# Five small moves in the order of an attention and feed-forward kernel: warming products, first loads, squares, output stores, one cast

## The chip, the cores and the metric

The kernel runs on one core of a Trainium2 chip. The metric is the device time of one execution in microseconds (us). A core has five engines that run side by side, each through its own list of instructions in order: TensorE (PE: matrix products, with its weight loads shown as PEld), VectorE (DVE), ScalarE (ACT), GpSimd (POOL) and SyncE (SP), which here issues nearly all DMA transfers. An instruction that has to wait holds up everything that stands behind it on its engine.

## The reference

```python
def reference(A_x, A_wqkv, A_wo, B_x, B_w1, B_w3, B_w2):
    xn = layernorm(A_x)                                   # 2048 tokens, D = 512
    q, k, v = split(xn @ A_wqkv)                          # 32 heads of 16
    p = softmax(where(0 <= i - j < 256, q @ k.T / 4, -1e9))
    s = (p @ v) @ A_wo
    h = silu(xn @ B_w1) * (xn @ B_w3)                     # F = 1792
    g = silu(h @ B_w2)
    return A_x + s * g                                    # float32 in and out
```

## The kernel before, in words

Every float32 operand of a large product is scaled by a power of two and written as the sum of two float16 parts (hi and lo), and three products (hi·hi, lo·hi, hi·lo) stand for one. The power of two for a block of weights comes out of the weights themselves: their squares are summed (`squares`, on ACT at L249 or on DVE at L251), the sums are cast to bfloat16 (`cast`, L261, on DVE), a small product with ones spreads them over the partitions (`powers`, L280 or L285, on PE), and a chain of small DVE instructions (L291 or L294 to L304) makes the scale. Then the weights are scaled and cut: on ACT and DVE (`split`, L333, L334) or on ACT and POOL (`split_pool`, L342, L343, L345).

The 2048 tokens go in four stretches of 512 (t = 0 to 3), the heads in four groups of eight (g). At the start the first stretch of x is normalised, turned on PE (L493) and cut into XH (ACT, L496) and XL (DVE, L501). `project` (L597) makes the queries (k = 0) and keys (k = 1) of a group, cuts them (L614 on ACT, L618 on DVE) and stores them to DRAM; `fetch` (L641) loads them back in the layout of the attention, keys into `KA` and queries into `qa`. `value` (L567, L570) makes the values. Attention runs by units (t, g, p), where p takes half of a group's heads: `pass1` (L665 on PE, L679 on DVE) finds each row's maximum, `pass2` (L746 scores, L756 exponentials on ACT, L774 the product with the values) does the rest.

The feed-forward part is the filling between these batches: `gate_up` (L1036) for the 14 blocks of 128 columns of w1 and w3, `down` (L1261) for w2, and a form with fewer products for the last two stretches (L1179). In the first stretch the blocks are also loaded (L868, L913), measured two at a time (`measure`; `measure_down` for w2, L923) and cut. `total` (L1313) makes the final product with wo and the stores of the output (L1324).

PSUM is used as two banks `m` for dense products (`bank()` takes them in turn), two double banks `s` (`scores_bank()`) and one `po`. A product into a bank waits until the reader of the bank's previous content is done.

What sets the order: PE's instructions stand in the order in which the code is written. `later(n, f)` puts a piece of work n steps ahead, a step being a batch of attention or a piece of dense work. `beside_scores(n, f)` attaches a scale's small products to a pass1 row, n steps ahead. DVE, ACT, POOL and SP get their order from a scheduler that goes by priorities and its own estimate of when inputs are there, so an edit in one place can move instructions in another. The places of the change:

- `keep_busy(4)` at L1561 runs four products of ones into a bank `m` while the cuts of x are being made; `k00` and `q00` at L1564 are the first two projections, `k00` into an `s` bank.
- `later(1, lambda: fetch(0, 0))` at L1573 loads the first keys and queries in four transfers of 192 KB, each with four heads.
- `qk[3][0]()` at L1589 loads the query and key weights of group 3 in two transfers (L395); `later(6, qk[3][1])` takes their squares.
- At L1369 `measure(6, 1)`, the squares of blocks 6 and 7, is put 5 steps later.
- At L267 the cast of squares taken one per `apart` steps comes at `apart * (len(parts) + 1) + 1`. That is 6 steps for the blocks (four parts, apart 1) and 11 for wo (four parts, apart 2).
- At L1329 the output store comes 4 steps after its product, for all but the last stretch.

Of the kernel before, what the change touches and what calls it, by code (L numbers as in the profile page):

```python
# [83 lines left out]
def tile_block(ctx: ExitStack, tc: tile.TileContext, x, wqkv, wo, w1, w3, w2, out):  # L84
# [59 lines left out]
    def later(n, f):  # L144
        made_so_far[0] += 1
        queue.append((now[0] + n, made_so_far[0], f))
# [16 lines left out]
    def bank(shape, dtype=F32):  # L163

        open_bank[0] = b = 1 - open_bank[0]
        return psm.tile(shape, dtype, name=f"m{b}", tag=f"m{b}", bufs=1)

    def scores_bank():

        return pss.tile([P, 2, 512], F32, name="s")  # L170
# [11 lines left out]
    def beside_scores(n, f):  # L182

        later(n, lambda: besides.insert(0, f))
# [55 lines left out]
    def squares(parts, on_act=0, apart=0):  # L240


        ssq = small.tile([P, len(parts)], F32, name="ssq")

        def one(i, raw):

            sq = ppool.tile([P, D], BF16, name="sqa" if i < on_act else "junk", bufs=1)
            if i < on_act:
                nc.scalar.activation(sq, raw, AF.Square, accum_out=ssq[:, i:i + 1])  # L249
            else:  # L250
                nc.vector.tensor_tensor_reduce(out=sq, in0=raw, in1=raw, scale=1.0, scalar=0.0,  # L251
                                               op0=ALU.mult, op1=ALU.add, accum_out=ssq[:, i:i + 1])
        for i, raw in enumerate(parts):
            if apart:
                later(apart * (i + 1), lambda i=i, raw=raw: one(i, raw))
            else:
                one(i, raw)
        sb = small.tile([P, len(parts)], BF16, name="sb")

        def cast():  # L260
            lasts["cast"] = nc.vector.tensor_copy(sb, ssq)  # L261
        def behind_bank():

            with tc.issue_after(lasts["emptied"].ins) if "emptied" in lasts else nullcontext():
                cast()
        if apart:
            later(apart * (len(parts) + 1) + 1, behind_bank)  # L267
        else:
            cast()
        return sb  # L270
# [310 lines left out]
    def project(t, g, k, terms=(range(3),), scores_bank=False):  # L581


        cell = {}

        parts = ([[(c, i) for c in (2 * half, 2 * half + 1) for i in range(3)] for half in range(2)] if len(terms) == 1
                 else [[(c, i) for i in group for c in range(NC)] for group in terms])

        def part(n):
            assert turned[t] == 4  # L590
            w = WQ[t, g, k]
            xh, xl = X[t]
            if n == 0:
                cell["pp"] = pss.tile([P, 2, TW], F32, name="s")[:, 0, :] if scores_bank else bank([P, TW])
            for c, i in parts[n]:
                a, b = ((0, xh), (1, xh), (0, xl))[i]
                nc.tensor.matmul(cell["pp"], w[:, (a * NC + c) * P:(a * NC + c + 1) * P], b[:, c, :], start=(c, i) == parts[0][0],  # L597
                                 stop=(c, i) == parts[-1][-1])
            if n < len(parts) - 1:
                return  # L600
            if t == 0:
                def store():
                    with behind_load():
                        nc.sync.dma_start(dWQ[g, k], w)
                    give(w, after=8)
                later(45, store)
            else:
                give(w)
            pp = cell["pp"]
            both = take(F16)  # L610
            B = both.rearrange("p (a t) -> p a t", a=2)
            s = QS / (XS * WS)
            with urgent():
                nc.scalar.activation(B[:, 0, :], pp, AF.Copy, scale=s)  # L614

            def rest():
                with urgent():
                    lasts["emptied"] = nc.vector.scalar_tensor_tensor(B[:, 1, :], pp, s, B[:, 0, :], op0=ALU.mult, op1=ALU.subtract)  # L618
                d = (dQ, dK)[k][g][:, :, t * TW:(t + 1) * TW]
                if k == 0:  # L620
                    nc.sync.dma_start(d[:, 0:2, :], B[:, 0:1, :].to_broadcast([P, 2, TW]))
                    nc.sync.dma_start(d[:, 2, :], B[:, 1, :])
                else:
                    nc.sync.dma_start(d[:, 0:2, :], B)
                    nc.sync.dma_start(d[:, 2, :], B[:, 0, :])
                give(both, after=4)
            later(1, rest)
        return opening([(len(l), lambda n=n: part(n)) for n, l in enumerate(parts)])
# [2 lines left out]
        WQ[t, g, k] = w = take(F16)  # L631
        nc.sync.dma_start(w, dWQ[g, k])

    def fetch(t, g):
        QA[t, g] = qa = qpool.tile([P, 4, TW], F16, name="qa")
        ka = keys(t, g)
        c0 = 0 if t else 2 * P
        for dst, d in ((ka[:, :, c0:], dK[g][:, :, t * TW - 2 * P + c0:(t + 1) * TW]),
                       (qa, dQ[g][:, :, t * TW:(t + 1) * TW])):
            for r in range(2):  # L640
                lasts["load"] = nc.sync.dma_start(dst[64 * r:64 * r + KR],  # L641
                                  d[64 * r:64 * r + 64].rearrange("(a d) i t -> (d i) a t", d=DH))

# [224 lines left out]

    measured = set()

    def measure(f, apart=0):

        raws = [RAW.pop(f + i) for i in range(2)]
        sb = squares([raws[0][0], raws[1][0], raws[0][1], raws[1][1]], on_act=4 if f > 2 else 2, apart=apart)

        def scale(s=None):
            pp = small.tile([P, 2, 2], F32, name="pp")
            pi = small.tile([P, 2, 2], F32, name="pi")  # L880
            return then(s, powers(sb, 4, pp.rearrange("p a b -> p (a b)"), pi.rearrange("p a b -> p (a b)"), s),
                        lambda: rest(pp, pi))

        def rest(pp, pi):
            ff = slice(f, f + 2)
            nc.vector.tensor_scalar(sg_scale[:, ff], pp[:, 0, :], 0.5 / (WS * XS), None, op0=ALU.mult)
            nc.vector.tensor_mul(p13[:, ff], pp[:, 0, :], pp[:, 1, :])
            measured.update((f, f + 1))

            def cut(i, k):  # L890
                if k == 0:
                    WF[0, f + i] = [[None, None], WF.pop((0, f + i), [None, None])[1]]
                WF[0, f + i][0][k] = a = take(F16)
                split_pool(a[:, 0:D], a[:, D:], raws[i][k], pi[:, k, i:i + 1])
                give(raws[i][k], after=5)
            for i in range(2):
                for k in range(2):
                    later(((1, 2, 4, 6) if f < 8 else (1, 5, 9, 13))[2 * i + k], lambda i=i, k=k: cut(i, k))
        if started:
            beside_scores(8, scale)  # L900
        else:
            later(10 if apart else 6, scale)

# [389 lines left out]
    def total(t, b):  # L1293
# [4 lines left out]
        def part(half):  # L1298
# [16 lines left out]
            if half:  # L1315
                with urgent():
                    lasts["emptied"] = nc.vector.scalar_tensor_tensor(y, ps, sc["y"], y, op0=ALU.mult, op1=ALU.mult)
                if t == NT - 1:
                    nc.vector.tensor_add(y, y, XR[t, b])
                else:  # L1320
                    halves(nc.gpsimd.tensor_add, y, y, XR[t, b])

                def store():
                    nc.sync.dma_start(out[r, :], y)  # L1324
                    give(y, XR[t, b], after=30)
                if t == NT - 1:
                    store()
                else:
                    later(4, store)  # L1329
                if b == 3:  # L1330
                    give(*(OT[t, g] for g in range(NG)))
        return opening([(6, lambda h=h: part(h)) for h in range(2)])
# [22 lines left out]
    def feed_forward():  # L1355
# [4 lines left out]
        for t in range(NT):  # L1360
            for f in range(FB):
                if t == 0:
# [3 lines left out]
                    elif f + LEAD == FB - 1:  # L1366
                        pieces += [(0, lambda f=f: load(0, f)) for f in range(FB - 2, FB)]
                    if f % 2 and f + 3 < FB:
                        pieces.append((0, lambda f=f + 3: later(5, lambda: measure(f, 1)) if f == 6 else measure(f, 1)))  # L1369
                    pieces += [(0, lambda f=f: load_down(0, f)) for f in range(f + 2 if f else 0, min(f + 3, FB))]  # L1370
                    for m in range(f + 1 if f else 0, min(f + 2, FB)):
                        k = next(k for k, (_, f1) in enumerate(GROUPS) if m < f1)
# [158 lines left out]
        nc.gpsimd.memset(KA[2][:, a, :].bitcast(F32), TWO_ONES)  # L1531


    def keep_busy(n):
        ps = bank([P, 4, P])
        for _ in range(n):
            nc.tensor.matmul(ps, onesb, onesb.unsqueeze(1).to_broadcast([P, 4, P]), start=True, stop=True)

# [19 lines left out]
        flush()  # L1558
    with tc.issue_after(lasts["hi"].ins), tc.issue_after(lasts["x"].ins):
        qk[1][1]()  # L1560
    keep_busy(4)  # L1561


    k00, q00 = (project(0, 0, k, ((0,), (1,), (2,)), k) for k in (1, 0))  # L1564
    run([k00[0], q00[0], k00[1]])
    qk[1][2]()
    with tc.issue_after(lasts["scale"].ins):
# [2 lines left out]
    qk[1][3]()  # L1570
    with tc.issue_after(lasts["hi"].ins):
        run([k00[2], q00[2]])
    later(1, lambda: fetch(0, 0))  # L1573
    k01 = project(0, 1, 1, ((0, 2), (1,)))
    run(k01[:1])
    wv[2]()
# [4 lines left out]
    sc["o"] = scaled(SQ["wv"][3], OS / WS, "so")  # L1581
    with tc.issue_after(lasts["hi"].ins):
        measure(0)
    run(project(0, 1, 0, scores_bank=True))
    later(1, lambda: fetch(0, 1))
    run(value(0, True))
    qk[2][1]()
# [89 lines left out]
```

## Time and profile before

| | |
|---|---|
| Time, median of 3 runs | 811.51 us (811.10 to 811.94) |
| The profiled execution, its own time | 811.24 us |
| Its span, first to last instruction | 809.4 us |
| PE busy | 793.7 us (98%) |
| DVE busy | 631.2 us (78%) |
| ACT busy | 392.1 us (48%) |
| POOL busy | 377.1 us (47%) |
| DMA queue of SP, share of 16 engines | 54.6% |
| Granted TensorE clock, mean | 1.00 |

The span lies 1.8 us below the execution's own time, which has the start and the end around it. Lines of a timeline below give start in us, duration in us, engine, line, operation, output and inputs, shapes and, in brackets, the engine's idle time just before with what ended it.

### The profile page before, as it was taken

Reading aid. Unit: us, or ns where it says so; the run is one execution under the profiler, and the core shown is the slowest. Engines: PE = TensorE matmul, PEld = TensorE weight load, DVE = VectorE, ACT = ScalarE, POOL = GpSimd, SP = SyncE. Lnnn points to the kernel's source line nnn. Section 1 sums busy time; section 2 is a strip of 40 time slices with the busy share of each in tenths; the row PEclk is TensorE's granted clock in tenths of the full one; section 3 lists DMA queues with packets and bytes.
Section 4 is the critical chain, followed back from the end, with each engine's and each line's share of the span. In section 5 each row is a group of like instructions: output and inputs, shape, how many; then the busy total and the mean of one; then the engine's idle time right before and its main releaser. Section 6 shows DMA issues by size and latency. Waiting matters only on the chain.

```text
span 809.4 us, 23944 instructions
## 1 busy us (share of the span) xinstructions
PE 793.7 (98%) x9176; PEld 403.7 (50%) x9176; DVE 631.2 (78%) x2037; ACT 392.1 (48%) x591; POOL 377.1 (47%) x732
## 2 busy tenths in 40 slices
PE   8999989999999999999999999999999999999998
PEld 4444444444444444444444454456544754466465
DVE  8788788887888777887988888777778787875437
ACT  6879586553546544345344433344444234344411
POOL 2345376342329445354353455530346276550670
PEclk9999999999999999999999999999999999999999
DMA  9968554835576474757655634646372644335321
GB/s 282 265 214 267 160 183 134 278 114 191 160 199 208 134 232 139 218 142 263 160 162 181 194 104 119 185 137 179 105 201 74 160 139 137 113 90 172 111 65 62
DMA packets 109795, 134.19 MB, mean 166 GB/s; under 512 B 18864, under 2 KB 64880, under 8 KB 109680
## 3 DMA queue, kind: packets, MB, share of 16 engines
q1 hardware_dynamic: 109392, 132.13, 54.6%
q8 instruction: 72, 1.18, 0.6%
q10 hardware_dynamic: 288, 0.52, 0.2%
q14 instruction: 43, 0.35, 0.1%
HBM read 91.23 MB, written 36.57 MB: 158 GB/s over the span
## 4 chain that ended last, share of the span: by engine, by line
PE 79%; DVE 8%; ACT 6%; DMA 3%; issue 2%; SPq 1%; POOL 0%; ACTq 0%; DVEq 0%
PE m L1036 30%; PE po L774 8%; PE m L1261 8%; PE m L1179 8%; PE m L597 7%; PE s L746 5%; PE m L1313 4%; PE m L567 4%; PE s L665 3%; DMA slot<-in_B_w_dram 2%; DVE junk L679 2%; PE po L665 2%; ACT slot L342 1%; ACT pt L756 1%; ACT sqa L249 1%
## 5 line engine op out<-in xcount | busy, mean ns | idle before, releaser
L1036 PE MATMUL m<-XH,slot 128*128 128x512 f16 x896 | 267.4, 380 | 1.6 <-DVE slot L618 1.2
L756 ACT ACTIVATE pt<-s,es 128x1024 f32<-128x1024 f32 x152 | 167.5, 1112 | 193.7 <-DVE s L753 186.5
L1036 PEld LDWEIGHTS <-slot 128*128 128x128 f16 x1344 | 124.7, 98 | 156.0 <-issue 12.0
L1036 PE MATMUL m<-XL,slot 128*128 128x512 f16 x448 | 169.9, 379 | 0.0
L753 DVE TENSOR_TENSOR s<-s,MK 128x256 f32<-128x256 f32 (+2 forms) x280 | 118.7, 434 | 51.2 <-PE s L746 47.0
L679 DVE CUSTOM_DVE_ANT_0 junk<-s,MW 128x320 bf16<-128x320 f32 x276 | 133.9, 485 | 17.9 <-PE s L665 10.3
L339 POOL TENSOR_TENSOR slot<-slot,slot 128x256 f16<-128x256 f32 (+1 forms) x86 | 57.7, 692 | 141.9 <-ACT slot L1069 76.7
L345 POOL TENSOR_TENSOR slot<-slot,slot 128x128 f16<-128x128 f32 x168 | 69.1, 446 | 58.3 <-ACT slot L343 58.3
L679 DVE CUSTOM_DVE_ANT_0 junk<-po,MW 128x320 bf16<-128x320 f32 x172 | 83.4, 485 | 4.7 <-DVE mt L704 0.3
L1261 PE MATMUL m<-slot,slot 128*128 128x512 f16 x336 | 78.6, 380 | 0.3 <-DVE slot L1055 0.3
L774 PE MATMUL po<-pt,V 64*32 64x320 f32 (+4 forms) x2880 | 77.2, 342 | 0.8 <-DVE pp L304 0.8
L597 PE MATMUL m<-XH,slot 128*128 128x512 f16 x240 | 71.0, 380 | 1.6 <-DVE slot L1055 1.2
L1179 PE MATMUL m<-slot,slot 128*128 128x256 f16 x588 | 68.4, 273 | 0.0
L1094 POOL TENSOR_TENSOR slot<-slot,slot 128x256 f16<-128x256 f32 x98 | 64.6, 671 | 1.1
L1051 ACT ACTIVATE slot<-m,sgs 128x512 f32<-128x512 f32 x56 | 38.3, 683 | 54.4 <-PE m L1036 52.3
L774 PEld LDWEIGHTS po<-pt,V 64*32 64x32 f32 x2880 | 50.5, 106 | 22.9 <-PE s L515 0.9
L1179 PEld LDWEIGHTS <-slot 128*128 128x128 f16 x588 | 56.1, 98 | 11.5 <-issue 3.0
L1055 DVE SCALAR_TENSOR_TENSOR slot<-slot,m 128x512 f32<-128x512 f32 x56 | 38.3, 684 | 29.0 <-ACT slot L1051 29.0
L746 PE MATMUL s<-qa,KA 50*64 50x320 f16 (+3 forms) x1472 | 58.4, 260 | 0.1
L597 PEld LDWEIGHTS <-slot 128*128 128x128 f16 x384 | 35.6, 98 | 44.8 <-issue 3.4
L746 PEld LDWEIGHTS <-KA 50*64 50x64 f16 x1472 | 30.1, 106 | 51.9 <-issue 30.9
L1261 PEld LDWEIGHTS <-slot 128*128 128x128 f16 x336 | 30.7, 98 | 38.6 <-issue 4.2
(189 smaller groups left out, 1138.5 us busy)
## 6 DMA issues: line engine op xcount, KB each, us to landing
slot<-dW SPq DMA_DIRECT2D x98, 256.0 KB
slot<-in_B_w_dram SPq DMA_DIRECT2D x56, 256.0 KB
slot<-dFold SPq DMA_DIRECT2D x48, 256.0 KB
dW<-slot SPq DMA_DIRECT2D x42, 256.0 KB
slot<-in_A_x_dram SPq DMA_DIRECT2D x30, 256.0 KB
KA<-dK SPq DMA_DIRECT2D x24, 288.0 KB
qa<-dQ SPq DMA_DIRECT2D x32, 192.0 KB
slot<-dWQ SPq DMA_DIRECT2D x24, 256.0 KB
```

Source lines behind the costliest of these rows:

```text
L339: op(out[:, c], a[:, c], b[:, c])
L345: nc.gpsimd.tensor_sub(lo[:, c:c + P], raw[:, c:c + P], hi[:, c:c + P])
L597: nc.tensor.matmul(cell["pp"], w[:, (a * NC + c) * P:(a * NC + c + 1) * P], b[:, c, :], start=(c, i) == parts[0][0], stop=(c, i) == parts[ ...
L679: lasts["maximum"] = nc.vector.tensor_tensor_reduce(out=junk[:, :n], in0=s[:, r, :n], in1=mask, scale=1.0, scalar=NEG, op0=ALU.add, op1=AL ...
L746: nc.tensor.matmul(s[64 * h:64 * h + 64, r, o:o + 64 * n], ka[rows, 2 * p + a, 64 * (m + 4):64 * (m + 5)], qa[rows, 2 * p + a, 64 * (m + k ...
L753: nc.vector.tensor_add(v, v, MK[:, kind, of:of + n, :].unsqueeze(1).to_broadcast([P, 2 * len(which), n, 64]))
L756: lasts["exp"] = nc.scalar.activation(pt, s, AF.Exp, scale=es)
L774: nc.tensor.matmul(cell["po"][32 * i:32 * i + 32, h, 64 * (m + k):64 * (m + k + n)], V[64 * h:64 * h + 64, (4 * t + m // 2) % VB, hd * VW: ...
L1036: nc.tensor.matmul(cell[k], w[:, (a * NC + c) * P:(a * NC + c + 1) * P], b[:, c, :], start=c == 0 and i == 0, stop=c == NC - 1 and i == 2)
L1094: nc.gpsimd.tensor_sub(lo, view, hi)
L1179: nc.tensor.matmul(cell["ps"][:, c], made[:, f:f + P], wj[:, g:g + 256], start=j == j0 and c == 0 and n == 0, stop=j == j1 - 1 and n == 2, ...
L1261: nc.tensor.matmul(ps, hh[:, a * TW + b * P:a * TW + (b + 1) * P], w[:, c * D:(c + 1) * D], start=f == f0 and i == 0, stop=f == f1 - 1 and ...
```

## The change

```diff
@@ squares
         if apart:
-            later(apart * (len(parts) + 1) + 1, behind_bank)
+            later(apart * len(parts) + 2, behind_bank)
@@ project
             if n == 0:
-                cell["pp"] = pss.tile([P, 2, TW], F32, name="s")[:, 0, :] if scores_bank else bank([P, TW])
+                cell["pp"] = bank([P, TW]) if scores_bank is False else scores_bank()[:, 0, :]
@@ fetch
-    def fetch(t, g):
+    def fetch(t, g, ps=None):
         QA[t, g] = qa = qpool.tile([P, 4, TW], F16, name="qa")
         ka = keys(t, g)
         c0 = 0 if t else 2 * P
-        for dst, d in ((ka[:, :, c0:], dK[g][:, :, t * TW - 2 * P + c0:(t + 1) * TW]),
-                       (qa, dQ[g][:, :, t * TW:(t + 1) * TW])):
-            for r in range(2):
-                lasts["load"] = nc.sync.dma_start(dst[64 * r:64 * r + KR],
-                                  d[64 * r:64 * r + 64].rearrange("(a d) i t -> (d i) a t", d=DH))
+        for heads in (slice(0, 4),) if ps is None else [slice(2 * p, 2 * p + 2) for p in ps]:
+            for dst, d in ((ka[:, heads, c0:], dK[g][:, :, t * TW - 2 * P + c0:(t + 1) * TW]),
+                           (qa[:, heads, :], dQ[g][:, :, t * TW:(t + 1) * TW])):
+                for r in range(2):
+                    rows = slice(64 * r + DH * heads.start, 64 * r + DH * heads.stop)
+                    lasts["load"] = nc.sync.dma_start(dst[64 * r:64 * r + KR],
+                                      d[rows].rearrange("(a d) i t -> (d i) a t", d=DH))
@@ measure
-    def measure(f, apart=0):
+    def measure(f, apart=0, until=8):
...
-            beside_scores(8, scale)
+            beside_scores(until, scale)
@@ total
-                    later(4, store)
+                    later(10, store)
@@ feed_forward
-                        pieces.append((0, lambda f=f + 3: later(5, lambda: measure(f, 1)) if f == 6 else measure(f, 1)))
+                        pieces.append((0, lambda f=f + 3: later(8, lambda: measure(f, 1, 6)) if f == 6 else measure(f, 1)))
@@ the start
-    def keep_busy(n):
-        ps = bank([P, 4, P])
+    def keep_busy(n, ps=None):
+        ps = bank([P, 4, P]) if ps is None else ps
...
-    keep_busy(4)
-    k00, q00 = (project(0, 0, k, ((0,), (1,), (2,)), k) for k in (1, 0))
+    waiting = scores_bank()
+    keep_busy(3, waiting[:, 0, :].rearrange("p (k q) -> p k q", q=P))
+    k00, q00 = (project(0, 0, k, ((0,), (1,), (2,)), (lambda: waiting) if k else False) for k in (1, 0))
...
-    later(1, lambda: fetch(0, 0))
+    later(1, lambda: fetch(0, 0, (0, 1)))
...
-    run(project(0, 1, 0, scores_bank=True))
+    run(project(0, 1, 0, scores_bank=scores_bank))
```

The last ones before the first projection go into the bank that this projection then fills, three instead of four. The first keys and queries come in eight transfers, the four of the first pair of heads ahead. The squares of blocks 6 and 7 start three steps later, their scale one. The cast for the blocks stays at 6 steps; the one for wo moves from 11 to 10. The output stores come six steps later. Code lines in the changed kernel lie up to three higher.

PE's list is the same before and now but for the ones. On the other engines the scheduler moved more than the diff names. First SP, near the start: stores (`dK`, `dQ` written from a slot) and loads (`KA`, `qa`) of the first two groups, and L395, the weights of group 3. Before:

```order
25 L624 DMA dK_147<-slot_408 128x2x512
26 L622 DMA dQ_143<-slot_417 128x512
27 L395 DMA slot_551<-in_A_wqkv_dram 128x4x128
28 L625 DMA dK_148<-slot_462 128x512
29 L641 DMA KA_140<-dK_147 48x4x512 x2
30 L641 DMA qa<-dQ_143 48x4x512 x2
31 L624 DMA dK_148<-slot_462 128x2x512
32 L621 DMA dQ_144<-slot_495 128x2x512
33 L622 DMA dQ_144<-slot_495 128x512
34 L395 DMA slot_552<-in_A_wqkv_dram 128x4x128
35 L641 DMA KA_141<-dK_148 48x4x512 x2
36 L641 DMA qa<-dQ_144 48x4x512 x2
```

Now, on SP at the same place:

```order
27 L625 DMA dK_148<-slot_464 128x512
28 L643 DMA KA_140<-dK_147 48x2x512 x2
29 L643 DMA qa<-dQ_143 48x2x512 x2
30 L643 DMA KA_140<-dK_147 48x2x512 x2
31 L643 DMA qa<-dQ_143 48x2x512 x2
32 L624 DMA dK_148<-slot_464 128x2x512
33 L621 DMA dQ_144<-slot_497 128x2x512
34 L622 DMA dQ_144<-slot_497 128x512
35 L395 DMA slot_553<-in_A_wqkv_dram 128x4x128
36 L643 DMA KA_141<-dK_148 48x4x512 x2
37 L643 DMA qa<-dQ_144 48x4x512 x2
38 L395 DMA slot_554<-in_A_wqkv_dram 128x4x128
```

The two halves of the first loads stand together. Both weight loads of group 3 went back: the first from ahead of the first loads to behind the second group's stores, the second from ahead of the second group's loads to behind them.

Second, DVE, among the maxima of the first unit's pass1 (L679, now L681). `M` rows are maxima, the cast of 128x2 is that of group 3's squares. Before:

```order
96 L679 ISA junk,M<-s,M_106 128x256
97 L679 ISA M 128x1
98 L294 TENSOR_SCALAR al<-s 128x1
99 L261 CAST sb<-ssq 128x2
100 L679 ISA junk,M<-s,MW 128x320
101 L679 ISA M 128x1
102 L295 SCALAR_TENSOR_TENSOR al<-s,al 128x1
```

Now the same cast stands 18 rows further down on DVE, past a whole stretch of maxima and cuts:

```order
112 L334 SCALAR_TENSOR_TENSOR slot_723<-slot_206,sw_643,slot_723 128x512
113 L334 SCALAR_TENSOR_TENSOR slot_726<-slot_205,sw_643,slot_726 128x512
114 L1057 SCALAR_TENSOR_TENSOR slot_737<-slot_737,m_716 128x512
115 L681 ISA junk,M<-s,MW 128x320
116 L681 ISA M 128x1
117 L261 CAST sb<-ssq 128x2
118 L681 ISA junk,M<-s,MW 128x320
```

Rows 98 and 100 of the first piece now follow each other, and the cast comes behind the first product of gate and up (L1055, now L1057).

Third, ACT at the same time. L249 with `slot_551` and `slot_552` (now 553 and 554) are group 3's squares, L923 (L925) those of w2, L1051 (L1053) the gate's tanh, L1069 (L1071) the cast of a finished block. Before:

```order
44 L249 ACTIVATE sqa,ssq<-slot_551 128x512
45 L249 ACTIVATE sqa,ssq<-slot_552 128x512
46 L570 ACTIVATE V<-m_619,uv 128x32x16
47 L333 ACTIVATE slot_721<-slot_206,sw_641 128x512
48 L333 ACTIVATE slot_724<-slot_205,sw_641 128x512
49 L1051 ACTIVATE slot_735<-m_714,sgs 128x512
50 L923 ACTIVATE sqa,ssq_737<-slot_708 128x512
51 L923 ACTIVATE sqa,ssq_737<-slot_710 128x512
52 L1069 CAST slot_785<-slot_735 128x512
```

Now, from the same two scalings (L333) on:

```order
46 L333 ACTIVATE slot_723<-slot_206,sw_643 128x512
47 L333 ACTIVATE slot_726<-slot_205,sw_643 128x512
48 L1053 ACTIVATE slot_737<-m_716,sgs 128x512
49 L249 ACTIVATE sqa,ssq<-slot_554 128x512
50 L1071 CAST slot_787<-slot_737 128x512
51 L342 ACTIVATE slot_209<-slot_209,pi 128x512
52 L925 ACTIVATE sqa,ssq_739<-slot_710 128x512
53 L1053 ACTIVATE slot_833<-m_810,sgs 128x512
54 L925 ACTIVATE sqa,ssq_739<-slot_712 128x512
```

The second of group 3's squares moved behind the tanh, and the first two squares of w2 behind the cast of the finished block.

## The prediction

> **What bounds the kernel now.** I read the page's first part first, then the table of windows, the timeline of PE, and last the timelines of whoever is named in PE's waits.
>
> ```profile
> span 809.4 us, 23944 instructions
> PE 793.7 (98%) x9176; PEld 403.7 (50%) x9176; DVE 631.2 (78%) x2037; ACT 392.1 (48%) x591; POOL 377.1 (47%) x732
> ```
>
> PE is busy for 98% of the span. An edit that leaves PE's products alone, as this one does but for one product of ones, can only move PE's waits. Where are they? The columns below are window, its length, busy time (instructions) of PE, PEld, DVE, ACT and POOL, granted clock, DMA share and GB/s:
>
> ```profile
> 30.00:55.30 25.30, 24.08 (x173) 10.43 (x174) 19.92 (x96) 21.54 (x48) 13.65 (x32) 1.00 0.79 224
> 55.30:77.00 21.70, 20.37 (x164) 8.98 (x163) 18.86 (x69) 18.57 (x38) 12.85 (x25) 1.00 0.81 265
> 98.00:170.00 72.00, 66.34 (x811) 32.70 (x810) 60.47 (x227) 51.91 (x94) 42.03 (x101) 1.00 0.58 189
> 200.00:400.00 200.00, 199.84 (x2418) 95.00 (x2416) 163.31 (x529) 96.70 (x129) 98.52 (x177) 1.00 0.61 186
> ```
>
> From 200 to 400 us PE idles 0.16 us: nothing can be won there. From 30 to 77 ACT is busy 21.54 of 25.30 and 18.57 of 21.70, DVE nearly as much: here the cutting of weights sets the pace and PE waits now and then. All waits of PE on which the change can act, in order:
>
> ```profile
> 12.85 1.02 PE L1537 MATMUL m<-onesb 128*128 128x512 bf16 x4 [0.58 <-DVE XL L501]
> 13.71 1.03 PE L597 MATMUL s<-XH,slot 128*128 128x512 f16 x4
> 29.50 0.24 PE L665 MATMUL s<-KA,qa 48*64 48x128 f16 x1
> 30.15 0.30 PE L665 MATMUL s<-KA,qa 48*64 48x128 f16 x7 [0.41 <-DMA qa<-dQ]
> 30.50 0.39 PE L567 MATMUL m<-wvh,XH 128*128 128x512 f16 x1
> 53.92 0.38 PE L1036 MATMUL m<-XL,slot 128*128 128x512 f16 x1
> 55.33 0.59 PE L1036 MATMUL m<-XH,slot 128*128 128x512 f16 x2 [1.03 <-DVE slot L618]
> 73.69 1.46 PE L1261 MATMUL m<-slot,slot 128*128 128x512 f16 x6 [0.26 <-DVE slot L1055]
> 76.93 0.33 PE L665 MATMUL po<-KA,qa 48*64 48x320 f16 x4 [0.84 <-DVE M L679]
> ```
>
> **The ones (0.4 us).**
>
> ```profile
> 12.41 0.62 ACT L496 CAST XH<-s 128x512 f16<-128x512 f32 x1
> 15.67 0.16 DVE L261 CAST sb<-ssq 128x2 bf16<-128x2 f32 x1
> 16.30 0.19 PE L280 MATMUL s<-sb,onesb 128*128 128x1 bf16 x2
> 16.53 0.16 DVE L291 TENSOR_SCALAR al<-s 128x1 f32<-128x1 f32 x1 [0.70 <-PE s L280]
> ```
>
> Today the ones wait 0.58 us for a bank that DVE reads at L501, and the first projection starts behind them at 13.71. In the other bank they run right behind the transposes, and the projection needs only the last cut, 12.41 + 0.62 = 13.03. That is up to 0.68 us earlier. PE would then reach the small product L280 at 15.6, but its input comes from the cast that ends at 15.67 + 0.16 = 15.83. So 0.4 us is carried on (16.30 − 15.9), and DVE, which waited 0.70 us for L280, takes it along. One product of ones less is inside this.
>
> **The first loads (0.6 us).** PE meets pass1 at 29.50 and has done it at 30.50: 0.41 us of it is the wait for `qa`, and two shorter ones lie around it. Without them I put this row at 0.4 us, so 0.6 us is free, if the halves are there.
>
> ```profile
> 25.39 0.88 SPq L641 DMA_DIRECT2D qa<-dQ  x2
> 26.32 0.44 SPq L624 DMA_DIRECT2D dK<-slot  x1
> 27.88 0.82 SPq L395 DMA_DIRECT2D slot<-in_A_wqkv_dram  x1
> 30.87 0.84 SPq L641 DMA_DIRECT2D KA<-dK  x2
> ```
>
> From the end of the issue, 25.39 + 0.88 = 26.27, to the use at 30.15 are 3.9 us. Now the first half is issued some 0.5 us sooner (one issue is 0.44, and L395 and a store went behind it) and is half as long; PE arrives 0.4 us sooner. By the Trainium skill ("DMA: Bandwidth & Descriptors", section "Anatomy of one DMA", which is fitted on GpSimd's path) a transfer costs about 2.0 us fixed plus its bytes at 436 KB per us, so 96 KB instead of 192 KB would save 0.2 us, an estimate; by it small transfers are hardly faster, and the term would be 0.3 rather than 0.6. The trace's 3.9 us holds queueing that this formula lacks, since SP's queue stores, loads weights and loads `qa` at the same time. I keep 0.6, and let zero to 0.6 be the bounds. PE then runs about 1.0 us ahead from 30.5 on, which is worth nothing if it waits longer at 55.33.
>
> **The cast of group 3's squares (1.6 us): the main term.** PE waits at 55.33 for DVE's L618, and that comes at the end of this chain:
>
> ```profile
> DVE sb L261 <- ACT sqa L249: 5.2, 4, 1.8
> 35.73 0.15 DVE L294 TENSOR_SCALAR al<-s 128x1 f32<-128x1 f32 x1
> 37.47 0.17 DVE L261 CAST sb<-ssq 128x2 bf16<-128x2 f32 x1 [1.60 <-ACT sqa L249]
> 37.69 0.49 DVE L679 CUSTOM_DVE_ANT_0 junk<-s,MW 128x320 bf16<-128x320 f32 x1
> 39.47 1.34 ACT L333 ACTIVATE slot<-slot,sw 128x512 f16<-128x512 f32 x2 [1.45 <-DVE sw L302]
> 40.71 0.67 ACT L1051 ACTIVATE slot<-m,sgs 128x512 f32<-128x512 f32 x1
> 42.68 0.49 DVE L679 CUSTOM_DVE_ANT_0 junk<-s,MW 128x320 bf16<-128x320 f32 x1
> 44.27 0.69 DVE L1060 SCALAR_TENSOR_TENSOR slot<-m,slot 128x512 f32<-128x512 f32 x1
> 44.99 0.62 ACT L1069 CAST slot<-slot 128x512 f16<-128x512 f32 x1 [2.25 <-DVE slot L1060]
> 53.65 0.58 ACT L614 ACTIVATE slot<-m 128x512 f16<-128x512 f32 x1
> 54.59 0.69 DVE L618 SCALAR_TENSOR_TENSOR slot<-m,slot 128x512 f16<-128x512 f32 x1
> ```
>
> Of 5.2 us in four waits of this kind, one of 1.60 stands at 37.47. Behind it queue the maxima, the scale (L302) for which ACT's L333 idles 1.45 us, and the products L1055 and L1060 for which ACT's L1069 idles 2.25 us. Now the cast stands 18 rows later, and the maxima of 37.69 follow L294 at once, at 35.9: 1.8 us sooner. With the 0.4 that DVE brings, less 0.1 for a cast that goes between other maxima, the chain is 2.1 us ahead: L333 at 37.4, L1060 at 42.2, L1069 at 42.9. The up-product that L1060 reads also comes 1.0 sooner from PE, and 42.2 does not outrun it. From L1069 to L614 ACT runs 8.7 us without a wait, and as before 14 instructions stand there (two squares of w2 came in; a square and a scaling went out). So L614 comes at 51.6, and L618 ends at 53.2 rather than 55.28. PE's own arrival is 53.92 + 0.21 (0.59 for two less 0.38 for one) − 1.0 = 53.1. PE goes on at 53.25: 2.05 us sooner. These terms don't add: this one takes the place of the two before it, which only make sure that PE is not the later of the two. If they are nought, PE arrives at 54.1 and the gain here is 1.2.
>
> **From 55 to 77, and squares of 6 and 7 (−0.15 us).**
>
> ```profile
> 57.64 0.62 ACT L1069 CAST slot<-slot 128x512 f16<-128x512 f32 x1 [1.06 <-DVE slot L1060]
> 57.72 0.48 DVE L679 CUSTOM_DVE_ANT_0 junk<-s,MW 128x320 bf16<-128x320 f32 x1
> 70.43 0.64 ACT L249 ACTIVATE sqa<-slot 128x512 bf16<-128x512 f32 x1
> 71.81 0.89 DVE L334 SCALAR_TENSOR_TENSOR slot<-slot,sw,slot 128x512 f16<-128x512 f32 x1 [0.71 <-ACT slot L333]
> ```
>
> On ACT a square and a scaling by L342 now stand ahead of the L333 that follows L614, which holds DVE's L334 up by some 0.7 us (half of 1.34). ACT itself idles 1.06 us at 57.64 and can take that in; DVE's maxima of 57.72 come behind L334 and L1060, and part of the delay stays. I put them at 1.85 us sooner, 0.2 less than L618; the bounds are 1.35 (all of it stays) and 2.05. At 70.43 a square of blocks 6 and 7 stood ahead of the L333 for which DVE waited 0.71 us; it now stands behind. That would give up to 0.7 us, but the tanh and product (L1051, L1055) on which PE waits at 73.69 have as much ACT work ahead of them as before. I take none of it. The waits at 73.69 and 76.93 stay as they are, and PE passes 77 us 1.9 us sooner, with 1.0 and 2.05 as bounds.
>
> **Output stores and wo's cast (0).**
>
> ```profile
> SPq L1324 <- POOL slot L339: 22.6, 10, 4.4
> 237.54 0.16 DVE L261 CAST sb<-ssq 128x4 bf16<-128x4 f32 x1
> ```
>
> SP waited 22.6 us at output stores for POOL's work of later pieces, and its loads queue behind these waits. Six steps later the waits can go; but PE idles 0.16 us in 200, so the row with the cover prices it: nothing, either way. wo's cast ran without a wait at 237.54; earlier by a step, it is covered by the same rows.
>
> **Sum.** The profiled execution took 811.24 us, its span 809.4. 811.24 − 1.9 = 809.3. The median of the runs, 811.51, lies 0.27 above it; a run holds a little of that, and I take 809.4.
>
> **Rivals.**
> 1. *Part of it is taken back.* If the halves still land late, PE comes to 53.92 hardly sooner and 1.2 us remain; if ACT's extra square at 54 isn't absorbed, 0.7 of 1.9 goes and 1.2 remain as well; both leave 0.5. For it: the DMA engines are 79 and 81% busy in these windows. Off the median that is 810.3 to 811.0; chance 0.22.
> 2. *The other waits shrink too.* From 98 to 170 PE idles 72.00 − 66.34 = 5.7 us; squares and casts are moved there too by the scheduler. If a third goes: 807.5. Against it: I see no moved row on which those waits rest. Chance 0.10.
> 3. *No change.* Every reorder is swallowed by the 76.93 wait on maxima: 811.5, chance 0.07.
> 4. *Slower: group 3's weights come too late.* Their second load (L395), issued at 27.88, now stands behind four loads of the second group (30.87 + 2 × 0.84 = 32.55) and four more transfers of 0.44 in the queue, less its own place ahead of them: at about 33.9. With the same 3.9 us it lands at 37.8. ACT's square of it now stands directly behind L1051, which ends at 40.71 + 0.67 − 2.1 = 39.3, and DVE's cast at 42.68 − 2.1 = 40.6. To be in time it must land by 40.6 − 0.8 = 39.8, a margin of 2 us. From there each microsecond comes back one for one, as DVE's wait at L261: at 41.7 the gain is gone, and from 43.3, 9.4 us after its issue, the kernel is slower than can be missed. For it: in the window 30 to 55 the DMA engines are 79% busy at 224 GB/s, and the 3.9 us come from one case. Against it: an overrun of 5.5 us is more than the whole time that the loads of 25.39 take. Time 813.3, chance 0.13.
>
> **How the numbers follow.** The forecast has 0.48. About 0.2% (1.6 us) is what a measurement of this kernel can tell from no change: below 809.9 is faster, above 813.1 slower. Faster: forecast and rival 2, 0.58. Same: rivals 1 and 3, 0.29. Slower: rival 4, 0.13. The range goes from 807.8 (part of rival 2) to 811.9 (all of rivals 1 and 3), and leaves out rival 4 and the far end of rival 2, 2 in 10.
>
> **What would show it.** In the trace after: the first projection at 13.0 to 13.3; pass1 without a wait for `qa` near 29; no wait at DVE's L261 between 35 and 42; ACT's first L333 near 37.4; L618 ending near 53.2, and PE's wait there below 0.3 us; the waits near 72 and 75 as they were; 200 to 400 as full as before. Wrong would be: a wait of ACT for a DMA at the second square of group 3 near 39.3 (rival 4); PE still waiting for `qa` (rival 1); or L618 earlier and PE at 77 not.

## The result and the profile after

The changed kernel takes 809.74 us (median), the kernel before, beside it on the same chips, 811.31 us. The ratio is 0.9981 (95% interval 0.9974 to 0.9987): 1.6 us faster, 1.0 to 2.1 by the interval. The profiled execution took 809.42 us against 811.24, 1.82 us less. Forecast were 809.4 us, and 1.9 us less for the profiled execution.

The page's first part and the table of windows of the changed kernel (columns as before), the first two windows put where the same work now lies:

```profile
span 807.6 us, 23976 instructions
PE 793.4 (98%) x9175; PEld 403.8 (50%) x9175; DVE 631.2 (78%) x2037; ACT 392.1 (49%) x591; POOL 378.0 (47%) x732
```

```profile
29.21:53.56 24.35, 23.66 (x174) 10.37 (x170) 19.96 (x98) 20.95 (x46) 13.79 (x30) 1.00 0.89 244
53.56:75.14 21.58, 20.36 (x164) 8.99 (x163) 19.17 (x71) 19.34 (x37) 13.05 (x26) 1.00 0.75 249
198.00:398.00 200.00, 199.88 (x2419) 95.04 (x2416) 163.60 (x529) 96.71 (x129) 99.08 (x177) 1.00 0.61 187
```

These two windows were 25.30 and 21.70 us long before, so 0.95 and 0.12 us are won in them, 0.79 ahead of them. PE's timeline, the rows that answer to those of the prediction (code lines from L641 on lie two or three higher):

```profile
13.05 1.02 PE L597 MATMUL s<-XH,slot 128*128 128x512 f16 x4 [0.17 <-ACT XH L496]
29.06 0.60 PE L667 MATMUL s<-KA,qa 48*64 48x128 f16 x8
29.71 0.39 PE L567 MATMUL m<-wvh,XH 128*128 128x512 f16 x1
53.59 0.59 PE L1038 MATMUL m<-XH,slot 128*128 128x512 f16 x2 [0.62 <-DVE slot L618]
75.07 0.33 PE L667 MATMUL po<-KA,qa 48*64 48x320 f16 x4 [0.70 <-DVE M L681]
```

The first projection starts 0.66 us sooner (13.71 before). Pass1 has no wait for `qa` any more, and the products behind it start at 29.71 rather than 30.50: 0.79 us of lead. At 53.59 the lead is 55.33 − 53.59 = 1.74, at 75.07 it is 1.86 (76.93 − 75.07). Behind 235 it grows to 2.10 (338.11 in the kernel before, 336.01 here) by wo's cast, as experiment 4 shows, and PE's last products lead by 2.06 as well. The span is only 1.8 us shorter: from the issue of the last stores to its end it is 3.9 us here and 3.7 before. Between 30 and 55, on DVE and ACT:

```profile
34.94 0.15 DVE L294 TENSOR_SCALAR al<-s 128x1 f32<-128x1 f32 x1
40.39 0.17 DVE L261 CAST sb<-ssq 128x2 bf16<-128x2 f32 x1
42.10 0.69 DVE L1062 SCALAR_TENSOR_TENSOR slot<-m,slot 128x512 f32<-128x512 f32 x1
51.90 0.49 DVE L681 CUSTOM_DVE_ANT_0 junk<-po,MW 128x320 bf16<-128x320 f32 x1 [0.43 <-DVE al L298]
52.85 0.69 DVE L618 SCALAR_TENSOR_TENSOR slot<-m,slot 128x512 f16<-128x512 f32 x1
```

```profile
37.04 1.34 ACT L333 ACTIVATE slot<-slot,sw 128x512 f16<-128x512 f32 x2 [0.22 <-DVE sw L302]
38.95 0.62 ACT L249 ACTIVATE sqa<-slot 128x512 bf16<-128x512 f32 x1
51.46 0.59 ACT L614 ACTIVATE slot<-m 128x512 f16<-128x512 f32 x1
```

The cast of group 3's squares runs at 40.39 without a wait (1.60 us before). L333, the up-product (now L1062) and L614 come at 37.04, 42.10 and 51.46; the prediction had 37.4, 42.2 and 51.6. ACT's square at 38.95 did not wait for its load, so rival 4 did not come. New is DVE's pause of 0.43 us at 51.90, 0.08 before.

Leads of this kind compare one execution with another, and they carry a spread of their own: PE's first product of the transposes (L493), which stands ahead of all edits, starts at 10.31 in the kernel before and between 10.18 and 10.60 in the other traces, at 10.28 here.

### The profile page after: what moved, and what is told of

It is laid out like the page before. It is cut to its first block, busy times and chain, and to the rows that moved or that the text cites. A ratio compares the mean times of both kernels' runs of the same rounds, so it can differ in the third digit from the quotient of the medians.

```text
span 807.6 us, 23976 instructions
## 1 busy us (share of the span) xinstructions
PE 793.4 (98%) x9175; PEld 403.8 (50%) x9175; DVE 631.2 (78%) x2037; ACT 392.1 (49%) x591; POOL 378.0 (47%) x732
## 4 chain that ended last, share of the span: by engine, by line
PE 82%; ACT 5%; DVE 5%; DMA 5%; issue 2%; SPq 1%; POOL 0%; ACTq 0%; DVEq 0%
PE m L1038 30%; PE m L1263 9%; PE po L776 9%; PE m L1181 8%; PE m L597 7%; PE s L748 5%; PE m L1315 4%; PE m L567 4%; DMA slot<-in_B_w_dram 3%; PE s L667 3%; PE po L667 2%; ACT pt L758 1%; DVE junk L681 1%; ACT slot L342 1%; ACT sqa L249 1%
## 5 line engine op out<-in xcount | busy, mean ns | idle before, releaser
L681 DVE CUSTOM_DVE_ANT_0 junk<-s,MW 128x320 bf16<-128x320 f32 x276 | 134.1, 486 | 18.0 <-PE s L667 10.3
L339 POOL TENSOR_TENSOR slot<-slot,slot 128x256 f16<-128x256 f32 (+1 forms) x86 | 57.6, 692 | 138.8 <-ACT slot L1071 73.4
L681 DVE CUSTOM_DVE_ANT_0 junk<-po,MW 128x320 bf16<-128x320 f32 x172 | 83.5, 486 | 4.7 <-DVE al L298 0.4
L1053 ACT ACTIVATE slot<-m,sgs 128x512 f32<-128x512 f32 x56 | 38.3, 683 | 54.4 <-PE m L1038 54.1
L1057 DVE SCALAR_TENSOR_TENSOR slot<-slot,m 128x512 f32<-128x512 f32 x56 | 38.3, 685 | 28.4 <-ACT slot L1053 28.4
```

Source lines behind the costliest of these rows:

```text
L339: op(out[:, c], a[:, c], b[:, c])
L681: lasts["maximum"] = nc.vector.tensor_tensor_reduce(out=junk[:, :n], in0=s[:, r, :n], in1=mask, scale=1.0, scalar=NEG, op0=ALU.add, op1=AL ...
```

## The experiments

The theories in the expectations: **A** is the prediction (DVE's wait at the cast bounds PE at 55 us; the other three edits cost and bring nothing). **B**: the gain is PE's earlier arrival, the cast is by the way. **C** and **D** came up on the way.

| Kernel | Median, us | Kernel before, us | Ratio, 95% interval |
|---|---|---|---|
| changed kernel | 809.74 | 811.31 | 0.9981 (0.9974 to 0.9987) |
| ones alone | 811.22 | 811.65 | 0.9996 (0.9987 to 1.0005) |
| halves alone | 812.38 | 811.65 | 1.0007 (0.9998 to 1.0017) |
| cast alone | 811.23 | 811.65 | 0.9992 (0.9983 to 1.0001) |
| other three edits alone | 811.43 | 811.65 | 0.9999 (0.9990 to 1.0008) |
| ones and halves | 811.04 | 811.48 | 1.0000 (0.9983 to 1.0017) |
| halves and cast | 811.95 | 811.48 | 1.0004 (0.9995 to 1.0012) |
| changed, without ones | 811.54 | 811.32 | 1.0001 (0.9992 to 1.0010) |
| changed, without halves | 810.52 | 811.32 | 0.9989 (0.9980 to 0.9998) |
| changed, without output stores | 810.93 | 811.46 | 0.9993 (0.9984 to 1.0002) |
| changed, without wo's cast | 810.11 | 811.46 | 0.9984 (0.9975 to 0.9993) |
| changed, without squares | 809.99 | 811.46 | 0.9983 (0.9974 to 0.9991) |
| changed, w2's cuts later | 809.18 | 811.48 | 0.9975 (0.9966 to 0.9985) |

No edit alone does what all of them do: the first four rows below the changed kernel are all within 0.1% of the kernel before, and their intervals hold 1. The traces show why. The wide interval of ones and halves comes with one execution of 818.41 us; the other ten took 810.32 to 811.92.

**1. Ones alone**

```diff
-    keep_busy(4)
+    waiting = scores_bank()
+    keep_busy(3, waiting[:, 0, :].rearrange("p (k q) -> p k q", q=P))
...
```

(with the other pieces of the diff that let the first projection take this bank)

> The kernel before with only the edit of the ones. In its order the cast of group 3's squares also goes behind the first scale and product, so two terms are in it. Theory A (DVE's wait at that cast sets the end at 55 us; ones and first loads only decide when PE arrives there): first projection at 13.05, the wait at L261 gone, PE's wait at 55 gone or small since PE comes there about 0.5 us sooner; gain 1.5 to 1.8 us. Theory B (the gain is PE's earlier arrival, from ones and first loads, and the cast is by the way): 0.4 to 0.6 us.

Measured: 0.4 us by the medians, with an interval on both sides of none. A's 1.5 to 1.8 is missed; B has the number, but not the way to it. PE's timeline and one row of DVE:

```profile
29.98 0.30 PE L665 MATMUL s<-KA,qa 48*64 48x128 f16 x7 [0.55 <-DMA qa<-dQ]
54.43 0.59 PE L1036 MATMUL m<-XH,slot 128*128 128x512 f16 x2 [0.85 <-DVE p2qk L304]
529.31 1.02 PE L1313 MATMUL m<-slot,slot 128*128 128x512 f16 x4 [0.63 <-DVE slot L1055]
```

```profile
525.01 0.35 DVE L821 RECIPROCAL dr<-dr 128x32 f32<-128x32 f32 x1 [3.91 <-DMA dr<-os]
```

Most of the lead of 0.5 us from the ones goes at pass1, with a longer wait for `qa` (0.55, 0.41 before); at 54.43 PE is 0.90 us ahead, since the wait at the cast is gone. In this execution all of it is lost again at 529.31, where PE waits for DVE, which had waited 3.91 us for a small load.

**2. Halves alone** (the `fetch` and `later(1, ...)` pieces of the diff alone)

```diff
-    later(1, lambda: fetch(0, 0))
+    later(1, lambda: fetch(0, 0, (0, 1)))
```

> The kernel before with only the first loads in halves. The cast of group 3's squares moves by one small instruction only, behind L295. Theory A: pass1 0.6 us sooner without the wait for qa, but DVE still waits over 1 us at L261, PE waits longer for L618, and 0 to 0.6 us is gained. Theory B: 0.6 to 1.4 us is gained, since PE's row runs on early.

```profile
37.07 0.40 DVE L261 CAST sb<-ssq 128x2 bf16<-128x2 f32 x1 [0.58 <-ACT sqa L249]
```

```profile
55.19 0.59 PE L1038 MATMUL m<-XH,slot 128*128 128x512 f16 x2 [1.29 <-ACT slot L333]
```

The first row is DVE's, the second PE's. Pass1 came sooner, and then PE waited 1.29 instead of 1.03 us at 55: 0.14 us of lead is left. Up to there A is right and B wrong. The time is 0.7 us above the kernel before by the medians, which neither foresaw. In this trace PE loses it far behind the edit: at 281.48 and 327.21 it waits 0.39 and 0.42 us for maxima, none in the kernel before (experiment 10 has the same two), and at 529.98 0.50 us behind the small load of experiment 1. PE also ran at half its rate near 120 us, but that cost nothing: the waits of the kernel before at 124.50 and 130.37 took it in, and the product of 130.37 starts at 130.22 here.

**3. Cast alone**

```diff
-    later(6, qk[3][1])
+    later(9, qk[3][1])
```

> The kernel before with group 3's squares three steps later (6 to 9), and nothing else: both squares go behind the tanh and the cast behind the first scale and product; ones, loads and SP's list are those of before. Theory A: no wait at L261 near 37, L333 near 37.7, L618 ends near 53.5, PE arrives itself at 54.1, gain 1.0 to 1.2 us. Theory B: 0 to 0.3 us.

DVE's timeline, then PE's row at 55:

```profile
35.92 0.15 DVE L294 TENSOR_SCALAR al<-s 128x1 f32<-128x1 f32 x1
43.05 0.69 DVE L1060 SCALAR_TENSOR_TENSOR slot<-m,slot 128x512 f32<-128x512 f32 x1
52.90 0.49 DVE L679 CUSTOM_DVE_ANT_0 junk<-po,MW 128x320 bf16<-128x320 f32 x1 [0.46 <-DVE al L298]
53.85 0.69 DVE L618 SCALAR_TENSOR_TENSOR slot<-m,slot 128x512 f16<-128x512 f32 x1
```

```profile
54.59 0.59 PE L1036 MATMUL m<-XH,slot 128*128 128x512 f16 x2 [0.77 <-DVE slot L618]
```

The wait at the cast is gone and 0.74 us is gained at 55 (B's 0 to 0.3 is missed), 0.4 by the medians. A's 1.0 to 1.2 is missed too: L294 ran 0.19 us later than before, the up-product came 1.22 us sooner, and the same pause on DVE (0.46) took 0.4 of that.

**4. The other three edits alone** (`later(10, store)`, wo's cast, squares of 6 and 7)

> The kernel before with the other three edits together: squares of blocks 6 and 7 later, output stores later, wo's cast a step sooner. Theory A: 0, within 0.2 us; SP's waits at L1324 below 22.6 us. The rival (SP's waits at the stores held loads up that PE needed): 0.4 us or more gained behind 200 us.

Measured: 0.2 us by the medians with an interval on both sides of none. A's bound holds, for these three alone. In the table of waits SP waited 16.3 us for POOL at L1324, 22.6 before, and PE has nothing of it at the load of dWQ, which was in time before. Of wo's cast it has something. PE's rows, first in the kernel before, then here:

```profile
237.39 0.31 PE L665 MATMUL s<-KA,qa 48*64 48x320 f16 x4
237.75 0.28 PE L285 MATMUL s<-sb,onesb 64*64 64x1 bf16 x12
```

```profile
237.80 0.31 PE L665 MATMUL s<-KA,qa 48*64 48x320 f16 x4
237.94 0.29 PE L285 MATMUL s<-sb,onesb 64*64 64x1 bf16 x14
```

From the pass1 products to the small product that needs the cast it is 0.36 us before and 0.14 here: 0.2 us won, as in the changed kernel. The count of PE's idle time hid most of this wait, since the row of 237.39 counts as busy until 237.70. In this trace the 0.2 is lost again at 529, where PE is 0.3 us later against the kernel before.

**5. Ones and halves**

> The kernel before with two edits: the ones and the first loads in halves (the cast moves with them). If the other three edits are worth nothing, this is the changed kernel: PE 1.7 us ahead at 55, 1.5 to 1.9 us gained. If they are worth something, it stays at 1.2 us or less.

DVE's cast for wo, SP's rows and PE's row:

```profile
236.11 0.16 DVE L261 CAST sb<-ssq 128x4 bf16<-128x4 f32 x1
```

```profile
334.29 0.43 SPq L632 DMA_DIRECT2D slot<-dWQ  x1
```

```profile
53.79 0.59 PE L1038 MATMUL m<-XH,slot 128*128 128x512 f16 x2 [0.64 <-DVE slot L618]
337.29 0.60 PE L597 MATMUL m<-XH,slot 128*128 128x512 f16 x2 [0.46 <-DMA slot<-dWQ]
```

By the expectation's own rule the other three edits are worth something: 0.4 us is gained by the medians, not 1.5 to 1.9. PE is 1.54 us ahead at 53.79 (55.33 − 53.79), nearly as in the changed kernel, and 0.82 at 337.29 (338.11 − 337.29), where it waits 0.46 us for weights whose load was issued only 3.0 us earlier.

**6. Halves and cast**

> The kernel before with the first loads in halves and group 3's squares three steps later (6 to 9), without the edit of the ones. Theory A (as predicted: at 55 PE needs only to arrive, and DVE's chain is 2.1 us ahead once the cast is away): PE arrives near 53.5, gain there 1.7 to 1.9 us. Theory C (new: the maxima ahead of L618 on DVE wait for PE's own pass1 rows at 52, so L618 comes as much sooner as PE is ahead there, and loads and ones count one for one): PE is 0.9 to 1.1 us ahead at 51.5, gain 1.1 to 1.4 us. Theory B (the cast does not matter, loads alone): 0.1 to 0.4 us as with the halves alone.

PE's timeline, then PE's table of windows (window, length, busy time, granted clock, DMA share, GB/s):

```profile
53.77 0.59 PE L1038 MATMUL m<-XH,slot 128*128 128x512 f16 x2 [0.38 <-DVE slot L618]
75.61 0.33 PE L667 MATMUL po<-KA,qa 48*64 48x320 f16 x4 [1.19 <-DVE M L681]
```

```profile
74.00:76.00 2.00, 0.72 (x9) 1.00 1.01 301
76.00:78.00 2.00, 2.00 (x6) 0.50 0.92 319
78.00:80.00 2.00, 2.00 (x8) 0.65 1.08 270
```

At 53.77 the lead is 1.56 us, between C's 1.1 to 1.4 and A's 1.7 to 1.9. Then PE waits 1.19 us at 75.61, and the granted clock falls to 0.50: PE makes 6 products in 2 us. (2.00 × 0.50 + 2.00 × 0.35) = 1.7 us are lost, all of the lead. Not every execution has this: six of the eleven have a mean clock of 0.997 or 0.998 and took 811.95 to 812.92 us, five have 0.999 or 1.00 and took 810.78 to 811.44, 0.0 to 0.7 under the kernel before. Waits of 0.39 and 0.42 us at 282.04 and 327.76, as with the halves alone, take more of the lead in this trace. C falls on another row: PE's pass1 rows, for which the maxima were to wait at 52, were done at 49.4 here. The maxima waited for nothing of PE's there.

**7. to 9. The changed kernel without one of the three**

```diff
-                    later(10, store)
+                    later(4, store)
```

> The changed kernel with the output stores 4 steps later as before (not 10). Theory D (new: these stores are worth nothing alone, but once PE is ahead the load of the query and key weights, dWQ, that queues behind a store's wait on SP comes too late): the load for the product at 336 is issued near 332 to 334 rather than 325, PE waits 0.2 to 0.6 us for it, and 0.2 to 0.6 us of the gain is lost. Theory A (the price of nothing in the prediction): as the changed kernel, within 0.2 us.

SP's timeline and PE's row:

```profile
333.64 0.34 SPq L1326 DMA_DIRECT2D out_dram<-slot  x1
334.02 0.43 SPq L632 DMA_DIRECT2D slot<-dWQ  x1
```

```profile
337.10 0.61 PE L597 MATMUL m<-XH,slot 128*128 128x512 f16 x2 [0.53 <-DMA slot<-dWQ]
```

For comparison SP's rows of the kernel before, and of the changed kernel:

```profile
332.59 0.34 SPq L1324 DMA_DIRECT2D out_dram<-slot  x1
332.97 1.52 SPq L632 DMA_DIRECT2D slot<-dWQ  x1
```

```profile
325.44 0.51 SPq L632 DMA_DIRECT2D slot<-dWQ  x1
333.24 0.34 SPq L1326 DMA_DIRECT2D out_dram<-slot  x1
```

D holds. With the old stores this load stands behind one of them on SP: it comes at 334.02, 3.1 us ahead of its use, and PE waits 0.53 us. With the new ones it comes at 325.44, 10.6 us ahead of 336.01. In the kernel before it was issued 5.1 us ahead (338.11 − 332.97), and PE did not wait. Here and in experiment 5 the load is there 3.1 and 3.0 us after its issue, so some 2 us were to spare before (an estimate from these rows). PE's lead of 1.7 us alone would not have used that up. But the store also comes 1.05 us later than before (333.64 against 332.59): it waits for additions on POOL (L339), and these end at 333.6 here and at 332.6 before, because four other additions that followed them before now go ahead of them. Both together are more than 2 us. 1.0 us of the gain is lost without this edit by the medians, more than expected. PE's lead falls from 1.7 to 1.0 us at this load, and two waits of 0.1 to 0.2 us at 236 and 528 are in this trace as well.

```diff
-            later(apart * len(parts) + 2, behind_bank)
+            later(apart * (len(parts) + 1) + 1, behind_bank)
```

> The changed kernel with the cast of wo's squares at 11 steps as before (not 10). Theory D: the cast comes near 235.5 rather than 232.05, and the small product at 235.7 waits 0.2 to 0.3 us for it; that much of the gain is lost. Theory A: as the changed kernel, within 0.1 us.

```profile
236.15 0.16 DVE L261 CAST sb<-ssq 128x4 bf16<-128x4 f32 x1
```

```profile
236.36 0.28 PE L285 MATMUL s<-sb,onesb 64*64 64x1 bf16 x12 [0.19 <-DVE sb L261]
```

The cast ends 0.05 us ahead of the product that needs it, and PE waits 0.19 us. In the changed kernel it stands at 232.05, and PE doesn't wait. 0.2 us of the gain is lost by the medians, as D had it; the intervals of the two kernels overlap, so that the trace carries this, not the times.

> The changed kernel with the squares of blocks 6 and 7 as before (5 steps, scale 8). Theory D: PE's lead at 77 is 1.6 to 1.7 us as in the kernel with ones and halves alone, not 1.86; 0.1 to 0.2 us lost. Theory A: as the changed kernel, within 0.1 us.

0.1 us by the medians, inside the noise. PE is 1.78 us ahead at 75.15 (76.93 − 75.15) instead of 1.86. What this edit is worth stays open.

**10. The changed kernel without the ones; 11. without the halves**

> The changed kernel with the four ones in their old bank as before; with that the cast of group 3's squares goes back to 15 rows further up, behind L295. Theory C and D (DVE's chain through this cast bounds PE at 55; the other edits only keep what is won): PE 0.4 to 0.6 us ahead at 30 to 51 from the loads, 0.1 to 0.3 us at 55, and 0 to 0.3 us under the kernel before in the end; if PE runs at half its rate again after a long wait near 77 or 118, up to 0.6 us above it. Theory B (PE's earlier arrival is what counts): 1.0 us or more under it.

> The changed kernel with the first loads whole, as before; the ones and the cast's new place stay. Theory C and D: the wait for qa at pass1 takes back the ones' lead, PE is 0.7 ahead at 51.5 and 0.9 at 55 as with the ones alone, but now this is kept to the end, since the stores and wo's cast are in: 0.6 to 0.9 us under the kernel before, no wait at 338. Theory A (only arrival at 55 counts): 1.5 us or more.

PE's rows without the ones:

```profile
54.77 0.59 PE L1038 MATMUL m<-XH,slot 128*128 128x512 f16 x2 [1.27 <-ACT slot L333]
280.68 0.33 PE L667 MATMUL po<-KA,qa 48*64 48x320 f16 x4 [0.39 <-DVE M L681]
```

DVE's row ahead of the second:

```profile
279.59 0.49 DVE L681 CUSTOM_DVE_ANT_0 junk<-po,MW 128x320 bf16<-128x320 f32 x1 [0.50 <-DVE M L681]
```

Without the ones the cast is back ahead of the scale, PE waits 1.27 us at 54.77 and is 0.56 ahead (somewhat more than expected); a wait of 0.39 us at 280.68 and a like one at 326 take that. Both come behind a pause of DVE of the kind at 51.90, here of 0.50 us at 279.59, and they stand in all three kernels that have the halves without the ones and in no other (the last section has what the pauses share). Nothing is left by the times: B's 1.0 us or more is wrong. Without the halves 0.8 us is left, in the expected 0.6 to 0.9, and it is kept to the end.

**12. w2's cuts later**, a version that follows from PE's longest remaining wait (1.63 us at 116.58, for an exponential that stands on ACT behind two scalings and two cuts of w2)

```diff
-                later(1 + 2 * i, lambda f=f: cut(f))
+                later((4 if k == 1 else 1) + 2 * i, lambda f=f: cut(f))
```

> The changed kernel with the cuts of w2's blocks 4 to 7 three steps later (1, 3, 5, 7 to 4, 6, 8, 10). On ACT two squares go ahead of the first of these scalings (L342), which waited 0.88 us for its scale, and a scaling and a cut go behind the exponential (L758) for which PE waits 1.63 us at 116.6. That exponential starts at about 114.9 rather than 115.44. If PE's wait follows it, 0.4 to 0.6 us faster than the changed kernel, 2.0 to 2.4 us under the kernel before; if the product of down then waits for the cuts, nothing or slower.

The exponential and PE's row behind it, first in the changed kernel, then in this one:

```profile
115.44 1.09 ACT L758 ACTIVATE pt<-s,es 128x1024 f32<-128x1024 f32 x1
```

```profile
116.58 0.30 PE L667 MATMUL s<-KA,qa 48*64 48x256 f16 x4 [1.63 <-ACT pt L758]
```

```profile
114.90 1.09 ACT L758 ACTIVATE pt<-s,es 128x1024 f32<-128x1024 f32 x1
```

```profile
116.05 0.30 PE L667 MATMUL s<-KA,qa 48*64 48x256 f16 x4 [1.11 <-ACT pt L758]
```

The exponential comes 0.54 us sooner, PE follows by 0.53. At 809.18 us the kernel is 2.3 us under the kernel before and 0.6 under the changed one by the medians, as forecast; the intervals of the two against the kernel before overlap, so that the trace carries this too.

## Why the prediction was right, and where not

**Ones and loads: right.** 13.05 was forecast as 13.0 to 13.3, the wait for `qa` is gone. The lead at 30 is 0.8 us, not 1.0.

**The cast: right in kind, its sum by luck.** The prediction gave the chain 1.8 us from the cast and 0.4 from PE's lead, less 0.1, and said of the terms of the ones and the first loads that they don't add and only make PE not the later of the two. They do add. In the kernels without the wait at the cast the gain at the up-product (44.27 before) is PE's lead, as it shows at DVE's L294 (35.73 before), plus a constant: cast alone −0.19 and 1.22, changed kernel 0.79 and 2.17, so 1.41 and 1.38. In three more it is 1.34 to 1.38, and 1.08 in the changed kernel without halves. The two terms were mis-sized against each other: 1.4 for the cast (of its 1.60), where 1.7 stood, and 0.8 for the lead, where 0.4 stood. That is 2.2, where 2.1 stood. The step that failed is the sentence that 1.2 us would remain without ones and loads; the cast alone gave 0.74.

**55 us.** L614 came as forecast; L618 began at 52.85 instead of 52.5, since DVE paused 0.43 us at 51.90. So 1.74 instead of 2.05. From there to 75 the prediction took 0.15 to 0.2 us off, and 0.12 came on top: the waits at 73.69 and 76.93 did not stay as they were (0.26 and 0.84 before; now 0.18, 0.20 and 0.70 in three places). So 1.86 at 75, inside the bounds of 1.0 to 2.05 and close to the 1.9, again by two misses that cancel.

**Stores and wo's cast at nothing: the step that failed.** "The row with the cover prices it: nothing, either way" took a stretch in which PE idles 0.16 us in 200 as one in which nothing can be won or lost. For wo's cast that was wrong already in the kernel before. The row of 237.54 said it: the cast ended at 237.70, and the product that needs it ran at 237.75; without the wait for it PE goes on 0.2 us sooner (experiment 4). With PE ahead and the cast at its old place PE waits 0.19 us (experiment 8). For the stores nothing was to be won, but they keep what is won: with the old ones the load of dWQ comes later, PE comes earlier, and 0.7 us of the lead goes (experiment 7). So the sum was right because all edits went in together. No edit alone shows a gain clear of noise, and without the stores two thirds of the gain are gone. That 1.82 us came out where 1.9 stood is in part luck as well: 1.86 from the front, 0.2 from wo's cast at a price of nothing, and 0.2 lost behind the last store.

**Rivals.** 1: it did not come in the changed kernel. The parts did lose their lead, but at other rows than it names. 2: two of the waits between 98 and 170 moved by a few tenths, the sum did not. 3: the wait at 76.93 went from 0.84 to 0.70 us and swallowed nothing. 4: its load was issued at 32.98 rather than 33.9, and ACT's square did not wait.

## What to carry to other kernels

A full engine is not proof of slack behind it: for every transfer and every small instruction ahead of its work, read how long before its use it is there. A lead of 1.5 us is kept only if each of these margins is larger than that, and larger by what the edit itself delays. A short wait can hide from the count of idle time: compare the distance between the starts of two rows. Terms that feed the same chain add, even where each seems to be hidden by another, so an edit is judged together with those that keep what it wins. And an exchange of two instructions on a secondary engine may carry the gain: here the ones moved a cast by way of the scheduler's order.

## What the runs showed of the hardware

One row of PE's timeline of the kernel before, beside those of experiment 6:

```profile
118.47 0.30 PE L665 MATMUL s<-KA,qa 48*64 48x256 f16 x4 [1.62 <-ACT pt L756]
```

After the wait of 1.19 us at 75.61 PE ran at half its rate for 3.4 us (1.7 us lost at a clock of 0.50), and so it did near 120 us with the halves alone (mean clock 0.997); this wait of 1.62 us left the clock at 1.00. The Trainium skill ("TensorE: Matmul & The Clock Gate", section "What's actually happening") has a free-running window of about 3.4 us and half rate after an idle one. The length of the spell agrees. That a window must be idle does not: from 74 to 76 PE was busy for 0.72 of 2.00 us, and from 72.60 to 76.00 for 1.97 of 3.40. At which share the rate falls is not shown by these runs.

The small load `dr` from `os` kept DVE waiting 2.37 us in the changed kernel, 2.61 before and 3.91 with the ones alone, at the same place and with the same transfers issued ahead of it on SP; PE's wait at 528 to 530 follows it. In the 14 traces it goes from 1.43 to 3.91 us; PE loses 0.2 to 1.1 us there in the six with 3.04 us or more, and nothing in the eight with 2.76 or less. Edits alone and combined stand on both sides, so what one trace loses at 529 is not the price of its edit. Why DVE pauses 0.43 us at 51.90 in the changed kernel and not in the one before was not tested: PE's rows that it reads were done 3 us earlier. But the traces show a pattern. Number all of DVE's records in each trace in order of time, semaphore instructions included. In the 14 traces 28 of the pauses ahead of a maximum last 0.40 to 0.48 us, and 27 of these stand at a record whose number is 64 more than a multiple of 128. Twelve traces have a maximum at record 192, and all twelve pause there, near 52 us; the kernel before and the one with the other three edits alone have a semaphore instruction at 192, and do not pause there. The waits at 281 and 327 follow pauses at records 960 and 1088. In all, 62 maxima stand at such a number, so the place is not enough by itself. In these kernels an edit that shifts DVE's list by a few records brought or took away some 0.4 us in this way.
